# RWKV-7 attention and a SiLU MLP on one core: chunk 0 inverted alone, the inverse turned by VectorE

## The chip, the core and the metric
The kernel runs on one core of a Trainium2 chip. Time is the device time of one execution in microseconds. The median of six runs of the kernel before is 964.92 us (952.55 to 973.38). Engines are TensorE (PE), VectorE (DVE), ScalarE (ACT), GpSimd (POOL) and SyncE (SP). Each engine works through its own list of instructions in order; an instruction that waits holds all behind it. DMA transfers are issued from SP's list and ScalarE's list.

## What is computed
For 4 batches, 8 heads, 768 steps and 40 channels per head a state of 40 by 40 is read, decayed and updated at every step; the result goes through an MLP with SiLU.

```python
for t in range(S):
    y[:, :, t] = np.einsum('bhd,bhde->bhe', rt, state)
    Sa = np.einsum('bhde,bhe->bhd', state, at)
    state = state * wt[:, :, None, :] - np.einsum('bhd,bhe->bhde', Sa, bt)
    state = state + np.einsum('bhd,bhe->bhde', vt, kt)
x = y.transpose(0, 2, 1, 3).reshape(B * S, H * D)      # 3072 x 320
h = x @ w_in                                           # 320 x 2048
out = (h / (1 + exp(-h))) @ w_out                      # 2048 x 320
```

## The kernel before
The 768 steps are cut into 12 chunks (NN) of 64 steps (C). A chunk is worked on as two units (NM), each of two batches. Within a chunk the recurrence is a triangular system, so each chunk needs the inverse of a 64x64 triangle for each of 32 (batch, head) pairs. The stages, by the names in the code:

- `load`, `load_w`, `load_rv` fetch a unit's channels: a, kb (b and k side by side), w, then v, r. `load_weights` fetches a piece of the MLP's weights into a room. The weights arrive as 64-bit floats; `weights` converts a piece in five VectorE and three ScalarE instructions (L164 to L176). The first pieces' rooms share the buffers of gts.
- `pre` (`prepare(n)`) has `scale`: scan products of w (L253), their reciprocal (L255), then GpSimd multiplies a and kb by them (L256, L258), and ScalarE sums squares as a check (L261, L262). And `scores`: TensorE makes the pair products of a and b (`between`, L231), VectorE masks them into sb (L239), and sb goes to the DRAM tile md (L274) with one head per partition.
- `inverse` reads md back into mi (L305) for two chunks at once: 64 partitions for the even chunk, 64 for the odd. For each row, one multiply (L310) and one reduction (L316) on VectorE fill XI. For chunks 0 to 3 (`small`) the triangle is cut to blocks of 16 and there are 15 rows; later there are 31 rows on blocks of 32. `back` writes XI to the DRAM tile zd (L323), turns XI within each partition into mi by two copies (ScalarE L325, VectorE L326) and writes that to xd (L327).
- `merge` has `fetch`, which reads blocks from zd (L343) and xd (L347) into XT, with the step in the partition; `first`, which for chunks 0 to 3 begins with `sixteen` (pq L357, the VectorE mask into qq L365, po L371 and L380, VectorE L390) and makes pq L407; and `second` (po L424), the last of the inverse. qq has the buffer of tmp, which the rows of `inverse` use.
- `chain` is a unit's attention: `keys` (pt L473), `right` (pm L231, masked into sk, pr L495), `solve` (pu L517, pw L535), `read` (pl L571, masked into vl L579), `write` (pgy L603, state Gbd L616 and L620, output yx L625, stored in the DRAM tile xs), `turn` (pt L555).
- `moe` reads xs into xt and makes ph (L666, L671), the sigmoid sg (ScalarE L674), gts (VectorE L675) and po (L682).

`weave` mixes lists of such steps, and the scheduler of the framework then sets each engine's order from that. A tile name with bufs=1 is one buffer: its next use waits until the last reader of the use before is done. Eight semaphores serve the DMA transfers in turn, so a transfer's issue waits until the eighth before it has landed.

The part around the change is the run-up: chunks 0 and 1 are prepared (`prepare(0)`, `prepare(1)`), inverted together (`invert(1)`), then chunk 0's chain runs with chunk 0's `first` and `second` before `solve`, and chunk 1's merge between `read` and `write` of chunk 0 (`late`). The w tiles of the first four units lie in tmp, mi and xt besides their own buffer. RHS, Gbd, GT and XT are cleared on GpSimd between `prepare(0)` and `prepare(1)`.

Of the kernel before, what the change touches and what calls it, by code (L numbers as in the profile page):

```python
# [41 lines left out]
def kernel(  # L42
# [39 lines left out]
    for be in range(2):  # L82
# [18 lines left out]
    XI = XIf[:, 0 : 32 * 32].rearrange("p (s t) -> p s t", s=32)  # L101

    w0 = sb.tile([128, Q, C + 1], F32, name="w")
    early = [
        sb.tile([128, 32 * 32], F32, name=x)[:, 0 : Q * (C + 1)].rearrange("p (q t) -> p q t", q=Q)
        for x in ("tmp", "mi", "xt")
    ]
    for w in [w0] + early:
        nc.vector.memset(w[:, :, 0:1], 0.0)
    nc.vector.memset(one, 0.0)  # L110
# [69 lines left out]

    issued = {}

    def in_order(x):

        if "last" in issued:
            info = mybir.DependencyInfo(mybir.DependencyClass.NoSync, mybir.DependencyReason.DATA)
            tc.add_manual_dep(x.ins, issued["last"].name, info, reason="in order")
        issued["last"] = x.ins

    class Unit:  # L190
# [5 lines left out]
        return u  # L196


    def load(u):
        u.a = sb.tile([128, Q, C], F32, name="a", bufs=4)  # L200
        u.kb = sb.tile([128, Q, 2, C], F32, name="kb", bufs=6)
        B2 = slice(2 * u.m, 2 * u.m + 2)

        def part(n, x):
            for be in range(2):
                nc.sync.dma_start(
                    u.kb[:, P * be : P * be + P, n], x[2 * u.m + be, u.n].rearrange("p (q t) -> p q t", q=P)
                )

        nc.sync.dma_start(  # L210
            u.a.rearrange("p (b q) t -> p b (q t)", b=2), aT[B2, u.n].rearrange("b p c -> p b c")
        )
        part(1, bT)
        part(0, kT)

    def load_w(u, at, queue=nc.sync):
        u.w = at
# [30 lines left out]
    def pre(u, md):  # L248
        def scale():
            u.W = sb.tile([128, Q, C + 1], F32, name="W", bufs=6)  # L250
            for be in range(2):
                W, w = (x[:, P * be : P * be + P].rearrange("p q t -> p (q t)") for x in (u.W, u.w))
                nc.vector.tensor_tensor_scan(W, w, one.rearrange("p q t -> p (q t)"), 0.0, ALU.mult, ALU.add)  # L253
            R = u.w[:, :, 1 : C + 1]
            nc.vector.reciprocal(R, u.W[:, :, 1 : C + 1])  # L255
            nc.gpsimd.tensor_tensor(out=u.a, in0=u.a, in1=u.W[:, :, 0:C], op=ALU.mult)  # L256
            for n in (1, 0):
                nc.gpsimd.tensor_tensor(out=u.kb[:, :, n], in0=u.kb[:, :, n], in1=R, op=ALU.mult)  # L258
            junk = sb.tile([128, Q, C], mybir.dt.bfloat16, name="junk")
            c = 2 * (NM * u.n + u.m)  # L260
            nc.scalar.activation(out=junk, in_=R, func=AF.Square, accum_out=chk[:, c : c + 1])  # L261
            nc.scalar.activation(out=junk, in_=u.W[:, :, 1 : C + 1], func=AF.Square, accum_out=chk[:, c + 1 : c + 2])  # L262

        def scores():
            if u.m == 0:
                sbs[u.n] = sb.tile([128, NM, 2, P, C], F32, name="sb", bufs=2)
            between(u, 1, sbs[u.n][:, u.m])

            M = slice(u.m, u.m + 1) if u.n < 2 else slice(0, NM)
            for be in range(2 if u.n < 2 or u.m == NM - 1 else 0):  # L270
                for c in range(2):
                    at = 64 * (u.n % 2) + 16 * (2 * be + c)
                    r = C * be + 32 * c
                    nc.sync.dma_start(  # L274
                        md[at + 8 * M.start : at + 8 * M.stop].rearrange("q s t -> s q t"),
                        sbs[u.n][r : r + 32, M, :, :, 32 * c : 32 * c + 32].rearrange("s m j p t -> s (m j p) t"),
                    )
            k = NM * u.n + u.m + 1
            if 3 < k < NM * NN:
                load_w(units[k // NM][k % NM], w0)  # L280

        return [scale, scores]

    def small(n):
        return n < 4

    def inverse(md, N, queue):
        steps = []  # L290
        xd = dr.tile([128, 32, 32], F32, name="xd", bufs=2)
        zd = dr.tile([128, 32, 32], F32, name="zd", bufs=2)
        mif = sb.tile([128, 2 * SKIP], F32, name="mi")
        mi = mif[:, 0 : 32 * 32].rearrange("p (s t) -> p s t", s=32)
        I = 32 // N
        tmp = sb.tile([128, 32 * 32], F32, name="tmp")[:, 0 : I * N * N]
        tmp = tmp.rearrange("p (i s t) -> p i s t", i=I, s=N)

        def blocks(x):
            x = x.rearrange("p (i x) -> p i x", x=SKIP)[:, :, 0 : 16 * 32] if N == 16 else x[:, 0 : 32 * 32].unsqueeze(1)  # L300
            return x.rearrange("p i (s t) -> p i s t", t=32)

        X, M = blocks(XIf), blocks(mif)
        for h in range(2):
            nc.sync.dma_start(mi[64 * h : 64 * h + 64], md[64 * h : 64 * h + 64])  # L305

        def row(t):
            n = N - 1 - t
            part = tmp[:, :, 0:n, 0:n]
            nc.vector.tensor_tensor(  # L310
                out=part,
                in0=X[:, :, t + 1 : N, t + 1 : N],
                in1=M[:, :, t, t + 1 : N].unsqueeze(2).to_broadcast([128, I, n, n]),
                op=ALU.mult,
            )
            last = nc.vector.tensor_reduce(out=X[:, :, t + 1 : N, t], in_=part, axis=AX.X, op=ALU.add)  # L316
            mark["row"] = last.ins

        for t in reversed(range(N - 1)):
            steps.append(partial(row, t))  # L320

        def back():
            nc.sync.dma_start(zd, XI)  # L323
            turned = XI.rearrange("p t s -> p s t")
            nc.scalar.copy(out=mi[:, 0:16], in_=turned[:, 0:16])  # L325
            nc.vector.tensor_copy(out=mi[:, 16:32], in_=turned[:, 16:32])  # L326
            queue.dma_start(xd, mi)  # L327

        steps.append(back)
        return steps, xd, zd  # L330

    def merge(n, xd, zd, queue):
        X = XT[n % 2].rearrange("p m h t -> p (m h) t")
        N = NM * H
        box = {}
# [1 line left out]
        def fetch():  # L337
            for be in range(2):
                at = 64 * (n % 2) + 32 * be
                for c in range(2):  # L340
                    r = C * be + 32 * c
                    if c == 0 or small(n):
                        nc.sync.dma_start(  # L343
                            X[r : r + 32, :, 32 - 32 * c : 64 - 32 * c],
                            zd[at + 16 * c : at + 16 * c + 16].rearrange("q t s -> t q s"),
                        )
                    queue.dma_start(  # L347
                        X[r : r + 32, :, 32 * c : 32 * c + 32],
                        xd[at + 16 * c : at + 16 * c + 16].rearrange("q s t -> s q t"),
                    )  # L350

        def sixteen(s, pp):

# [360 lines left out]
            md[0] = dr.tile([128, 32, 32], F32, name="md", bufs=2)  # L714
        return [x for u in units[n] for x in pre(u, md[0])]

    def invert(n):

        if n >= NN or n % 2 == 0:
            return []  # L720
        box = {}
        queue = nc.scalar if n == 1 else nc.sync

        def begin():
            box["rows"], box["xd"], box["zd"] = inverse(md[0], 16 if small(n) else 32, queue)

        def do(k, i):
            if i == 0:
                box[k] = merge(k, box["xd"], box["zd"], queue)
            box[k][i]()  # L730

        late[n - 1] = [partial(do, n, 1), partial(do, n, 2)]
        return (
            [begin]
            + [lambda i=i: box["rows"][i]() for i in range(16 if small(n) else 32)]
            + [partial(do, n - 1, 0), partial(do, n, 0), partial(do, n - 1, 1), partial(do, n - 1, 2)]
        )

    def run(steps):
        for step in steps:  # L740
            step()

    for u, at in zip(units[0] + units[1], [w0] + early):
        load_w(u, at, nc.scalar)
        load(u)
    for n in range(5):
        load_weights(n, nc.scalar)
    convert = [partial(weights, n) for n in range(NW + 1)]

    xs = dr.tile([DM, 4 * NM * C], F32, name="xs", bufs=2)  # L750
    run(prepare(0))
    for t in RHS + Gbd + GT + XT:
        nc.gpsimd.memset(t, 0.0)
    run(prepare(1))
    steps = invert(1)
    run(steps[0:1])
    for u in units[0]:
        load_rv(u)
    chains = {0: [chain(u, xs) for u in units[0]]}
    run([x[i] for i in range(2) for x in chains[0]])  # L760
    run(convert[0:6] + steps[1:16])
    queue = []
    with tc.issue_after(mark["row"]):
        for u in units[2]:
            load(u)
        run(steps[16:])
        steps = [x for pair in zip(*[x[2:] for x in chains[0]]) for x in pair]
        steps[4:4] = late.pop(0)
        weave(steps, convert[6:21])
        for u in units[1]:  # L770
            load_rv(u)
        for u in units[3]:
# [187 lines left out]
```

## Time and profile before
| what | us |
|---|---|
| median of six runs | 964.92 |
| lowest, highest | 952.55, 973.38 |
| the profiled execution | 966.44 |
| its span (first to last instruction) | 964.7 |
| TensorE busy | 838.0 |
| VectorE busy | 532.1 |
| ScalarE busy | 289.7 |
| GpSimd busy | 97.1 |

The mean granted clock of TensorE is 0.906 of full speed. The profiled execution is 1.5 us above the median of the runs, and 1.7 us of it lie outside its span. In the lines below, a time in square brackets is how long the engine was idle before the instruction, and after the arrow stands what ended the wait. A group "x8" is eight instructions of one kind, and its duration runs from the first start to the last end. SPq and ACTq are the lists that issue transfers.

### The profile page before, as it was taken

The page shows a single profiled execution, that of the slowest core. Times are in us where ns is not written, and L with a number is a line of the kernel's source. Part 1 is how long each engine was busy: PE and PEld are TensorE (multiplying, and loading weights), DVE is VectorE, ACT ScalarE, POOL GpSimd, SP SyncE. Part 2 cuts the span into 40 slices and gives each one's busy share as a digit, 9 for nine tenths or more (in the row PEclk, how much of TensorE's full clock was granted, in tenths as well). Part 3 has the DMA queues.
Part 4 walks back from the last instruction along what each step waited for, and adds up shares of the span by engine and source line. Part 5 has one row for each costly group of instructions (what it writes and reads, how often), then busy time and mean ns, then how long its engine had stood idle before and what let it go on. Part 6 is the DMA issues. An engine that isn't in the chain of part 4 may idle for free.

```text
span 964.7 us, 26553 instructions
## 1 busy us (share of the span) xinstructions
PE 838.0 (87%) x11586; PEld 590.5 (61%) x11586; DVE 532.1 (55%) x1078; ACT 289.7 (30%) x660; POOL 97.1 (10%) x98
## 2 busy tenths in 40 slices
PE   0407899789989848999989999979999999999997
PEld 0407887556768723786645876627866468756544
DVE  8955588992106499146894167981549813031111
ACT  2435474522323112235212433113431133210110
POOL 5210010310001101002010012100020000000000
PEclk9855598799659669999999999999999999999999
DMA  9594556433114360355533365313542223002001
GB/s 229 112 233 115 138 153 157 114 84 88 47 38 115 82 150 12 77 141 118 119 76 77 84 149 125 84 31 86 129 96 74 95 48 76 2 8 67 1 1 30
DMA packets 235498, 88.30 MB, mean 92 GB/s; under 512 B 198640, under 2 KB 226544, under 8 KB 235376
## 3 DMA queue, kind: packets, MB, share of 16 engines
q1 hardware_dynamic: 225920, 83.14, 36.1%
q10 hardware_dynamic: 9456, 3.41, 1.7%
q8 instruction: 92, 1.51, 0.6%
q14 instruction: 30, 0.25, 0.1%
HBM read 69.21 MB, written 17.30 MB: 90 GB/s over the span
## 4 chain that ended last, share of the span: by engine, by line
PE 55%; DVE 31%; DMA 4%; issue 4%; SPq 2%; ACT 1%; POOL 1%; ACTq 0%; POOLq 0%; DVEq 0%
PE po L682 15%; PE ph L666 10%; DVE tmp L310 6%; DVE XI L316 6%; PE pl L571 5%; PE ph L671 4%; DVE w L255 3%; DVE W L253 3%; PE pq L407 3%; PE po L424 2%; PE pu L517 2%; DVE gts L675 2%; PE pm L231 2%; PE pr L495 2%; PE pt L473 2%
## 5 line engine op out<-in xcount | busy, mean ns | idle before, releaser
L682 PE MATMUL po<-wo_s,gts 128*128 128x320 f32 x768 | 225.0, 445 | 0.5 <-DVE gts L675 0.4
L666 PE MATMUL ph<-xt,wi_s 128*128 128x512 f32 (+1 forms) x448 | 195.4, 572 | 30.9 <-DVE gts L675 14.8
L682 PEld LDWEIGHTS po<-wo_s,gts 128*128 128x128 f32 x768 | 143.1, 192 | 62.0 <-issue 4.1
L666 PEld LDWEIGHTS ph<-xt,wi_s 128*128 128x128 f32 x448 | 83.1, 199 | 116.1 <-issue 57.7
L675 DVE TENSOR_TENSOR gts<-ph,sg 128x512 f32<-128x512 f32 (+1 forms) x112 | 65.8, 608 | 138.2 <-ACT sg L674 138.1
L674 ACT ACTIVATE sg<-ph 128x512 f32<-128x512 f32 (+1 forms) x112 | 54.8, 533 | 237.0 <-PE ph L671 236.9
L231 PE MATMUL pm<-a,kb 64*64 64x64 f32 x1536 | 48.7, 242 | 39.1 <-POOL kb L258 24.1
L310 DVE TENSOR_TENSOR tmp<-XI,mi 128x2 f32<-128x2 f32 (+35 forms) x154 | 77.5, 503 | 3.5
L258 POOL TENSOR_TENSOR kb<-kb,w 128x512 f32<-128x512 f32 x42 | 50.7, 1228 | 263.8 <-DVE w L255 195.1
L316 DVE TENSOR_REDUCE XI<-tmp 128x2 f32<-128x2 f32 (+35 forms) x154 | 71.6, 465 | 3.8
L231 PEld LDWEIGHTS pm<-a,kb 64*64 64x64 f32 x1536 | 39.8, 149 | 51.3 <-POOL kb L258 42.4
L239 DVE TENSOR_TENSOR sk<-pm,ms 128x256 f32<-128x256 f32 x48 | 18.1, 419 | 95.6 <-PE pm L231 95.5
L255 DVE RECIPROCAL w<-W 128x512 f32<-128x512 f32 x21 | 70.3, 3347 | 0.8
L671 PE MATMUL ph<-xt,wl_s 64*128 64x512 f32 (+1 forms) x224 | 63.2, 604 | 0.0
L256 POOL TENSOR_TENSOR a<-a,W 128x512 f32<-128x512 f32 x24 | 28.8, 1199 | 287.1 <-DMA a<-in_aT 203.3
L571 PEld LDWEIGHTS pl<-r,vut 64*128 64x128 f32 x768 | 52.3, 213 | 4.8 <-issue 2.1
L571 PE MATMUL pl<-r,vut 64*128 64x64 f32 x768 | 53.7, 299 | 1.3 <-DVE vl L579 1.2
L564 ACT COPY GT<-pt 40x512 f32<-40x512 f32 x44 | 25.5, 579 | 87.1 <-PE pt L555 86.5
L579 DVE TENSOR_TENSOR vl<-pl,ml 128x512 f32<-128x512 f32 x48 | 30.9, 685 | 24.3 <-PE pl L571 24.3
L239 DVE TENSOR_TENSOR sb<-pm,ms 128x256 f32<-128x256 f32 x48 | 18.1, 412 | 46.2 <-PE pm L231 46.1
L603 PE MATMUL pgy<-vl,kt 128*64 128x104 f32 (+1 forms) x768 | 41.9, 267 | 0.0
L671 PEld LDWEIGHTS ph<-xt,wl_s 64*128 64x128 f32 x224 | 19.2, 195 | 35.2 <-issue 34.0
(106 smaller groups left out, 1016.8 us busy)
## 6 DMA issues: line engine op xcount, KB each, us to landing
a<-in_aT SPq DMA_DIRECT2D x24, 256.0 KB
kb<-in_bT SPq DMA_DIRECT2D x48, 128.0 KB
kb<-in_kT SPq DMA_DIRECT2D x48, 128.0 KB
vut<-in_vT SPq DMA_DIRECT2D x48, 128.0 KB
r<-in_rT SPq DMA_DIRECT2D x24, 256.0 KB
w<-in_wT SPq DMA_DIRECT2D x40, 128.0 KB
room<-in_w_out SPq DMA_DIRECT2D x20, 256.0 KB
v<-in_v SPq DMA_DIRECT2D x48, 80.0 KB
```

The source lines that it names most:

```text
L231: nc.tensor.matmul(pm[j][C * be : C * be + C, p * C : p * C + C], lhsT=u.kb[J, q, n, :], rhs=u.a[J, q, :], start=True, stop=True,)
L255: nc.vector.reciprocal(R, u.W[:, :, 1 : C + 1])
L258: nc.gpsimd.tensor_tensor(out=u.kb[:, :, n], in0=u.kb[:, :, n], in1=R, op=ALU.mult)
L310: nc.vector.tensor_tensor(out=part, in0=X[:, :, t + 1 : N, t + 1 : N], in1=M[:, :, t, t + 1 : N].unsqueeze(2).to_broadcast([128, I, n, n]) ...
L316: last = nc.vector.tensor_reduce(out=X[:, :, t + 1 : N, t], in_=part, axis=AX.X, op=ALU.add)
L571: nc.tensor.matmul(pl[j][:, q * C : q * C + C], lhsT=u.vut[J, q].rearrange("p n t -> p (n t)"), rhs=u.r[J, q, :], start=True, stop=True,)
L603: nc.tensor.matmul(pgy[be][J, p * N + last * D : p * N + N], lhsT=u.kt[:, P * be + p, J], rhs=u.vl[:, P * be + p, j, last * D :], start=u. ...
L666: in_order(nc.tensor.matmul(ph[n], lhsT=wi_s[:, k, at : at + 128], rhs=xt[:, k, :], start=k == 0, stop=False))
L671: in_order(nc.tensor.matmul(ph[n], lhsT=wl_s[R, i, :], rhs=xt[R, 2, :], start=False, stop=True))
L674: nc.scalar.activation(out=sg, in_=ph[n], func=AF.Sigmoid)
L675: nc.vector.tensor_tensor(out=place(2 * i + n), in0=ph[n], in1=sg, op=ALU.mult)
L682: in_order(nc.tensor.matmul(po[:, 0:DM], lhsT=place(f)[:, b * 128 : b * 128 + 128], rhs=wo_s[:, NF // 2 * half + f, :], start=f == 0, stop ...
```

## The change
1. `inverse` takes partitions lo to hi. Chunk 0 is inverted alone in 64 partitions (`invert(0, 1)`) and then chunk 1 alone (`invert(1, 1)`); later chunks still go in pairs. Chunk 1's rows are issued after chunk 0's `second`, and its `first` and `second` come after `write` of chunk 0 and before `turn` (`steps[6:6]` for `steps[4:4]`).
2. zd is gone. `fetch` reads xd alone, and a 32x32 block transpose on VectorE makes the other orientation within XT: four per chunk for chunks 0 to 3, two per chunk later.
3. Clearing RHS, Gbd, GT and XT comes first on GpSimd.
4. Order and queues: md of chunks 0 and 1 is written by ScalarE's queue, once per chunk (8 transfers for 16), chunk 1's after mi of chunk 0 is issued. The first weight pieces come from SP behind the loads of chunks 0 and 1; b and k of chunk 2 are loaded earlier. For chunk 0 the k product on GpSimd and the check sums come after the scores (`keys`), and scans and reciprocals stay in program order. Four weight pieces are converted among chunk 0's rows, for six before.
5. The w tiles of the first units lie in buffers of sg and xt.

```diff
+    def behind(x, ins):
+        info = mybir.DependencyInfo(mybir.DependencyClass.NoSync, mybir.DependencyReason.DATA)
+        tc.add_manual_dep(x.ins, ins.name, info, reason="in order")
...
-            for n in (1, 0):
-                nc.gpsimd.tensor_tensor(out=u.kb[:, :, n], in0=u.kb[:, :, n], in1=R, op=ALU.mult)
+            nc.gpsimd.tensor_tensor(out=u.kb[:, :, 1], in0=u.kb[:, :, 1], in1=R, op=ALU.mult)
+            if u.n > 0:
+                keys()
...
-            M = slice(u.m, u.m + 1) if u.n < 2 else slice(0, NM)
-            for be in range(2 if u.n < 2 or u.m == NM - 1 else 0):
+            queue = nc.scalar if u.n < 2 else nc.sync
+            for be in range(2 if u.m == NM - 1 else 0):
...
+                    if u.n == 1:
+                        behind(x, mark["mi"])
...
-        for h in range(2):
-            nc.sync.dma_start(mi[64 * h : 64 * h + 64], md[64 * h : 64 * h + 64])
+        for h in range(lo, hi, 64):
+            mark["mi"] = queue.dma_start(mi[h : h + 64], md[h : h + 64]).ins
+        L = slice(lo, hi)
...
-            nc.sync.dma_start(zd, XI)
...
-                    if c == 0 or small(n):
-                        nc.sync.dma_start(
-                            X[r : r + 32, :, 32 - 32 * c : 64 - 32 * c],
-                            zd[at + 16 * c : at + 16 * c + 16].rearrange("q t s -> t q s"),
-                        )
...
+            for r in range(0, 128, 32 if small(n) else 64):
+                c = r % 64
+                nc.vector.transpose(out=X[r : r + 32, :, 32 - c : 64 - c], in_=X[r : r + 32, :, c : c + 32])
...
+    for t in RHS + Gbd + GT + XT:
+        nc.gpsimd.memset(t, 0.0)
     for u, at in zip(units[0] + units[1], [w0] + early):
         load_w(u, at, nc.scalar)
-        load(u)
-    for n in range(5):
-        load_weights(n, nc.scalar)
-    convert = [partial(weights, n) for n in range(NW + 1)]
-
-    xs = dr.tile([DM, 4 * NM * C], F32, name="xs", bufs=2)
-    run(prepare(0))
-    for t in RHS + Gbd + GT + XT:
-        nc.gpsimd.memset(t, 0.0)
-    run(prepare(1))
-    steps = invert(1)
-    run(steps[0:1])
+    for n in range(2):
+        for what in "ab", "k":
+            for u in units[n]:
+                load(u, what)
+    for n in range(3):
+        load_weights(n)
     for u in units[0]:
         load_rv(u)
+    for n in range(3, 5):
+        load_weights(n)
+    for u in units[2]:
+        load(u, "bk")
+    convert = [partial(weights, n) for n in range(NW + 1)]
+
+    xs = dr.tile([DM, 4 * NM * C], F32, name="xs", bufs=2)
+    steps = prepare(0)
+    run([steps[i] for i in (0, 3, 1, 4, 2, 5)])
+    rows = invert(0, 1)
+    run(rows[0:1])
+    run(prepare(1))
     chains = {0: [chain(u, xs) for u in units[0]]}
     run([x[i] for i in range(2) for x in chains[0]])
-    run(convert[0:6] + steps[1:16])
+    run(convert[0:4] + rows[1:17])
     queue = []
     with tc.issue_after(mark["row"]):
+        run(rows[17:])
+        rows = invert(1, 1)
+        run(late.pop(0))
+        run(rows)
         for u in units[2]:
-            load(u)
-        run(steps[16:])
+            load(u, "a")
         steps = [x for pair in zip(*[x[2:] for x in chains[0]]) for x in pair]
-        steps[4:4] = late.pop(0)
-        weave(steps, convert[6:21])
+        steps[6:6] = late.pop(1)
+        weave(steps, convert[4:21])
```

## The prediction
> **What bounds the kernel now.** I read the slices of the page first, then the table by windows, the timelines of TensorE and VectorE, and the chain of waits for the first 130 us.
>
> ```profile
> PE   0407899789989848999989999979999999999997
> DVE  8955588992106499146894167981549813031111
> PEclk9855598799659669999999999999999999999999
> ```
>
> A slice is 24.1 us. From about 385 us on TensorE is at 9 nearly everywhere: what is to be won lies before. Three places show it idle: the first 72 us, a loose stretch up to 220 us, slice 14.
>
> ```profile
> 53.00:73.00 20.00, 0.53 (x4) 0.35 (x4) 10.44 (x24) 7.92 (x22) 3.63 (x3) 0.50 1.01 217
> 89.00:103.00 14.00, 13.91 (x216) 13.71 (x219) 5.31 (x16) 9.18 (x25) 0.00 (x0) 0.50 0.56 140
> 170.00:195.00 25.00, 19.38 (x155) 12.90 (x154) 24.77 (x45) 13.04 (x35) 6.73 (x6) 0.80 0.51 121
> ```
>
> Columns: length; busy TensorE, weight load, VectorE, ScalarE, GpSimd; granted clock, DMA share, GB/s. In 53 to 73 us TensorE does nothing while the inverse travels through DRAM. At 170 to 195 us VectorE is full (24.77 of 25) and TensorE has holes.
>
> ```profile
> 37.32 3.85 DMA mi<-md
> 53.89 4.35 DMA xd<-mi
> ...
> 60.77 4.81 DMA kb<-in_bT
> 66.28 5.28 DMA room<-in_w_in
> ```
> ```profile
> 69.06 4.05 SPq L343 DMA_DIRECT2D XT<-zd  x8
> 78.23 0.48 DVE L365 TENSOR_SCALAR qq<-pq,lower 128x256 f32<-128x256 f32 x1
> 124.88 1.67 PE L555 MATMUL pt<-ident,Gbd 64*40 64x64 f32 x32 [0.95 <-DVE Gbd L620]
> 185.68 1.14 PE L231 MATMUL pm<-a,kb 64*64 64x64 f32 x32 [4.49 <-POOL kb L258]
> 187.76 2.07 PE L666 MATMUL ph<-xt,wi_s 128*128 128x256 f32 x4 [0.94 <-DVE gts L675]
> 356.42 5.73 PE L666 MATMUL ph<-xt,wi_s 128*128 128x512 f32 x8 [13.46 <-DMA xt<-xs]
> ```
>
> The scores come back at 41.2 us, 15 rows run to 52.7 us, xd lands at 58.2, but zd is issued only at 64.27 behind loads that wait on SP; its eight reads start at 69.06. The first step with the inverse on VectorE (L365) is at 78.23. From 124.88 us (the state turned, chunk 1 begins) to 220.6 us, where chunk 3's inverse is done, MoE work runs between the chunks.
>
> **The change, part by part.** The order of each engine's instructions in the changed program gives what stands behind what.
>
> 1. *Start and chunk 0's rows.* Per unit the same scan, reciprocal (3.3 us) and products are done. Memsets of some 5 us move ahead of GpSimd's products, where it idled 5.48 us: nothing. The six weight transfers leave the ScalarE queue for SP behind all loads, md (8 transfers for 16) leaves SP for ScalarE. At the start's 229 GB/s the 4.2 MB of channels and 0.8 MB of weights are in by 23 us, 1.7 MB of r and v by 31 us. Reciprocals end at about 10.8, 17.6, 23.8, 29.3 us (before: 30.0); md's four writes wait for the second unit's mask at 24.5 us. But mi<-md stands on ScalarE behind two key copies, which need TensorE after the fourth score: 34.2 us, landing near 38 (before: 41.2). Then chunk 0's first row stands on VectorE behind the second unit's sk, which needs pr of the first: 39.6 us. Chunk 1's four md writes wait on ScalarE for loads of SP until about 38.5 us; behind them stand only copies that are needed from 40 us on. Gain 1.7 us. Nine weight conversions (0.33 us apart: 3.0) now stand among the rows and one sk mask less: rows end at 53.7 instead of 52.7. Half the partitions save nothing, the row is as long.
>
> 2. *The way back.* xd is issued at 55.5 (after the copy, 1.07), lands at about 58.3 (128 KB; 2.3 to 4.4 us by xd's 4.35 under a full DMA). ScalarE issues four XT reads in place of eight, landed by 64. zd's write (6) and its 32 reads go away. In their place stand the transposes, four per merge, 32x512 each. No row has one; VectorE's copy of 512 columns (L326) takes 0.58. The Trainium skill speaks against it: "VectorE: DVE Perf Modes", section "The three transpose paths", has 311 ns for a 128x128 bf16 tile, so an estimate of 4 x 311 = 1.24 us for 512 columns. By the row four cost 2.4 us, by the rule 5.0, on the path for chunks 0 and 1: the sum is up to 5.2 us worse. I take 0.6, the nearest row (bounds 0.5 and 1.24); below nothing is excluded, it is added work. They stand behind ten conversions and chunk 2's scan and reciprocal (1.3 + 3.35) on VectorE: start 65.7, end 69.2; with 2.3 us of matmuls and six conversions L365's successor runs at 71.7. Gain **6.5 us**. The 16 + 16 later transposes stand where VectorE idles (19.88 us behind chunk 5's rows): nothing; without that cover 0.6 each, 14 us at most over the rest.
>
> 3. *Chunk 1 inverted on its own.* Fifteen more rows of two instructions: 41.3 to 52.7 less 0.75 of mask, 10.7 us on VectorE. Their tmp is the buffer of chunk 0's qq, so the first row waits for chunk 0's last merge matmul: 88.4 - 6.5 = 82 us. Between the rows stand 16 conversions (0.28 each: 4.5), four vl masks (2.6) that wait for pl (96.3), Gbd's and yx's updates (5.9): rows end at about 105. Then conversions (3), chunk 2's second scan and reciprocal (4.65) are still ahead of the transposes, so X is ready near 119, while xd and four reads (2.8 + 4 + 2) hide behind them. TensorE has pgy done at 99.6 and waits 20 us in order. Next is the merge, 14.3 us in the trace (102.76 to 117.09), plus 1.7 as a reciprocal of chunk 3 stands before its L390: the turn at 135 instead of 124.9. **+10 us**; with a transpose of 1.24, +13.
>
> 4. *What that wait buys.* VectorE meanwhile does chunk 2's second and chunk 3's two reciprocals (before at 135, 169 and 181 us), at an equal count of converted weights (21). The stretch to 220 us had TensorE waiting 4.49 + 0.94 us there, and 3.2 us of half-clock matmuls after it (L666 x4 took 2.07, 1.13 warm). That goes: -8.6. Of other stalls in the stretch (1.20 and 1.17 us behind VectorE, 3.0 of cold matmuls after the first) I count half: -2.7. Sum **-11.3 us**, bounds -5 and -16.
> The skill's rule on the clock ("TensorE: Matmul & The Clock Gate", Part 1: full rate after some 3.4 us of sustained work) would let denser solving at 67 to 99 us double its speed, -10 us more. The row 89.00:103.00 denies it: 13.91 of 14 us busy, clock 0.50. These small matmuls don't lift it; I count nothing there.
>
> 5. *Slice 14.* TensorE waits 13.46 us for xt<-xs, whose yx stands behind a reciprocal. In the changed TensorE order one 16-matmul po group of the MoE before and two ph matmuls come after the last turn of chunk 3, so they run in this hole: 16 x 0.29 + 0.5 = **-5.1 us** (bounds 0 and -8). The later order is nearly the same: nothing.
>
> Sum: -6.5 is spent inside +10; +10 - 11.3 - 5.1 = -6.4. Against the profiled execution (966.44 us, span 964.7) 960; the median of the runs is 1.5 lower than that execution, so 958.5; said as 959.
>
> **Rivals.**
> - *A, as summed* (0.47): chunk 1 late, given back by VectorE's slack and the filled hole. 954 to 964.
> - *B, larger gain* (0.27): VectorE is the true bound from 125 to 220 us. For: 91.91 of 103 us busy at 117 to 220, reciprocals on the chain of waits. Three gone with their scans are 14 us, and if conversions cost less among rows, X of chunk 1 comes 4 earlier: -6.4 - 4 - 4 = 952. Against: TensorE too is at 90.93 of 103.
> - *C, slower* (0.12): the second inversion is the bound. Its place is TensorE's queue at the first pq of chunk 1; +10 stays, relief only 5 and the hole as wide as before: 965 + 5 = 970; with transposes at the rule's price 973 to 976. It decides once X of chunk 1 is ready after some 128 us instead of 119. For: the tmp wait and 37 us of VectorE work between 82 and 119 in strict order.
> - *D, nothing gained* (0.14): each wait is taken over by the next, 963 to 967. The transposes may also not replace a wait: XT<-xd was there by 68 us, and the conversions kept VectorE to 78 anyway.
>
> **How the numbers follow.** 1% (9.6 us, about what tells a change from none here) is 955 and 974. Faster by more: most of B and a part of A's low end: 0.34. Slower by more: C's upper half and a little more: 0.09. The same: 0.57. The range takes A, most of B, D and C's lower part: 947 to 971.
>
> **What would show it.** Right: chunk 0's first row at 38 to 41 us, its transposes near 0.6 us and over by 70; L365's successor at 70 to 74; TensorE idle some 20 us before chunk 1's pq, VectorE busy then; no 4.49 us hole behind GpSimd near 185; the hole before xt<-xs under 10 us. Wrong: X of chunk 1 before 105 us (gain over 1%); transposes at 1.2 us; the clock at 1.0 in 70 to 100 us; VectorE waiting on XT reads in later chunks with gts queued behind.

## The result, and the profile after

| | before | after |
|---|---|---|
| median, first comparison | 964.72 us (37 runs) | 955.29 us (16 runs) |
| lowest, highest | 952.55, 976.72 | 949.11, 964.34 |
| profiled execution, its span | 966.44, 964.7 | 959.11, 957.0 |

The ratio is 0.9936 with a 95% interval of 0.9911 to 0.9960: 0.64% faster, inside the 1% that was said; the median is 3.7 us under the 959 us. The ratio takes only the fast runs of both kernels, those within 1.5% of the kernel's fastest, so it is not the quotient of the two medians (0.9902). A second comparison (run e11) gave 0.9865 (0.9821 to 0.9910), which is outside that 1%. The two intervals do not meet, so one comparison is less certain than its interval says. The change gains between half and one and a half per cent. The total came out as forecast; of its terms two did not, with opposite signs, and that the sum came so near is in part luck.

The slices of the changed kernel (tenths of busy time; PEclk is the granted clock):

```profile
PE   0518378989999979999989999989999999999996
...
DVE  8797888896226796264993367971649723031120
...
PEclk9855559889979999997999999999999999999999
```

Slices are counted from 0. TensorE's hole in slice 14 is smaller (7 for 4). PEclk was 6, 5, 6 and 6 in slices 10, 11, 13 and 14; now it is 9, 7, 9 and 9, and below 9 behind that only in slice 18 (7). The stretches that the prediction showed, in the columns it explained:

```profile
53.00:73.00 20.00, 3.42 (x186) 3.05 (x188) 19.61 (x45) 8.64 (x22) 4.53 (x5) 0.50 0.71 171
89.00:103.00 14.00, 14.00 (x179) 13.76 (x178) 11.19 (x31) 6.98 (x21) 0.00 (x0) 0.52 0.32 80
170.00:195.00 25.00, 24.71 (x333) 18.28 (x335) 22.62 (x54) 10.10 (x26) 2.20 (x2) 0.92 0.57 144
```

At 53 to 73 us VectorE is full (19.61 for 10.44) and TensorE has begun. At 89 to 103 us TensorE is as full as before and the clock still half. At 170 to 195 us VectorE is relieved (22.62 for 24.77) and TensorE has no large hole (24.71 for 19.38). In order of time:

```profile
40.64 0.15 DVE L316 TENSOR_TENSOR tmp<-XI,mi 64x2 f32<-64x2 f32 x1 [0.43 <-DMA mi<-md]
...
64.83 1.38 DVE L353 STREAM_TRANSPOSE XT<-XT 32x512 f32<-32x512 f32 x2
...
71.71 0.48 DVE L368 TENSOR_SCALAR qq<-pq,lower 128x256 f32<-128x256 f32 x1
...
84.00 0.16 DVE L316 TENSOR_TENSOR tmp<-XI,mi 64x2 f32<-64x2 f32 x1 [0.70 <-PE po L427]
...
123.75 0.71 DVE L353 STREAM_TRANSPOSE XT<-XT 32x512 f32<-32x512 f32 x1
```
```profile
121.74 0.25 PE L360 MATMUL pq<-XT,sb 16*32 16x16 f32 x2 [18.21 <-DVE XT L353]
...
138.20 3.64 PE L558 MATMUL pt<-ident,Gbd 64*40 64x64 f32 x64
...
184.07 0.68 PE L230 MATMUL pm<-a,kb 64*64 64x64 f32 x16 [0.29 <-ACT GT L567]
...
205.47 2.08 PE L669 MATMUL ph<-xt,wi_s 128*128 128x256 f32 x4 [2.77 <-DVE gts L678]
...
332.34 5.11 PE L685 MATMUL po<-wo_s,gts 128*128 128x320 f32 x18 [1.17 <-DVE gts L678]
339.89 3.70 PE L669 MATMUL ph<-xt,wi_s 128*128 128x512 f32 x8 [2.44 <-DMA xt<-xs]
```

The lines show chunk 0's first row (40.64), the transposes (0.70 us each), the first qq (71.71, before 78.23), and chunk 1's rows behind the last merge matmul (84.00). Then TensorE waits 18.21 us for chunk 1's inverse, and the state turns at 138.2 us. The hole of 4.49 us behind GpSimd near 185 us is 0.29; the one before xt<-xs, 13.46 us, is left as 1.17 and 2.44.

**Where the time went.** The page's rows of TensorE for before, after, and after once more (run e11):

```profile
PE 838.0 (87%) x11586; PEld 590.5 (61%) x11586; DVE 532.1 (55%) x1078; ACT 289.7 (30%) x660; POOL 97.1 (10%) x98
```
```profile
PE 830.8 (87%) x11586; PEld 585.8 (61%) x11586; DVE 567.4 (59%) x1141; ACT 291.2 (30%) x661; POOL 97.9 (10%) x98
```
```profile
PE 821.9 (87%) x11586; PEld 576.7 (61%) x11586; DVE 566.4 (60%) x1141; ACT 291.1 (31%) x661; POOL 97.6 (10%) x98
```

Span less busy time is TensorE's idle time: 964.7 - 838.0 = 126.7, 957.0 - 830.8 = 126.2, 948.3 - 821.9 = 126.4 us. It is the same. What fell is busy time for the same 11586 matmul records. The clock accounts for it: four ph matmuls took 2.07 us at half clock and 1.13 us at full clock, and with half of the time at half clock (122.6, 103.6 and 83.3 us) taken off, 776.7, 779.0 and 780.3 us of busy time are left. Cut at the same work, the second MoE stage's first po matmul (219.77 us before, 232.89 after), and with the clock record laid over the matmuls:

| us | idle, up to there | behind | busy at half clock, up to there | behind |
|---|---|---|---|---|
| before | 77.6 | 49.1 | 60.7 | 61.9 |
| after | 89.7 | 36.4 | 62.7 | 41.0 |
| after again | 88.9 | 37.6 | 62.8 | 20.5 |

The start gave 12 us of idle time more and the rest took it back; half of the fall in half-clock time (122.6 to 103.6 us: 9.5) is about what the shown execution won (7.7 of span). Between the two executions of the changed kernel, 8.7 us apart, hardly anything but the clock differs. The timed runs agree: their mean clock is 0.907 before (67 runs) and 0.922 after (20), and among the 67 the time and the mean clock of a run have a correlation of -0.93. A correlation shows no cause by itself; e5 below tests it.

### The profile page after: what moved, and what is told of

Same layout as the page of the kernel before. It is cut to its first block, busy times and chain, and to the rows that moved or that the text cites. A ratio compares the mean times of both kernels' runs of the same rounds, so it can differ in the third digit from the quotient of the medians.

```text
span 957.0 us, 26541 instructions
## 1 busy us (share of the span) xinstructions
PE 830.8 (87%) x11586; PEld 585.8 (61%) x11586; DVE 567.4 (59%) x1141; ACT 291.2 (30%) x661; POOL 97.9 (10%) x98
## 4 chain that ended last, share of the span: by engine, by line
PE 55%; DVE 31%; DMA 6%; issue 4%; SPq 2%; ACT 2%; POOL 1%; ACTq 0%; POOLq 0%; DVEq 0%
PE po L685 13%; PE ph L669 10%; DVE tmp L316 7%; DVE XI L322 6%; PE pl L574 5%; PE ph L674 3%; DVE w L255 3%; PE pq L410 3%; PE pu L520 3%; PE pt L476 2%; DVE gts L678 2%; PE pgy L606 2%; PE pr L498 2%; PE pm L230 2%; PE po L427 2%
## 5 line engine op out<-in xcount | busy, mean ns | idle before, releaser
L685 PE MATMUL po<-wo_s,gts 128*128 128x320 f32 x768 | 222.3, 442 | 3.1 <-DVE gts L678 3.0
L669 PE MATMUL ph<-xt,wi_s 128*128 128x512 f32 (+1 forms) x448 | 196.0, 572 | 21.4 <-DVE gts L678 17.6
L677 ACT ACTIVATE sg<-ph 128x512 f32<-128x512 f32 (+1 forms) x112 | 54.6, 533 | 232.6 <-PE ph L674 232.3
L316 DVE TENSOR_TENSOR tmp<-XI,mi 64x2 f32<-64x2 f32 (+40 forms) x169 | 80.9, 479 | 7.9 <-DMA mi<-md 3.5
L255 DVE RECIPROCAL w<-W 128x512 f32<-128x512 f32 x24 | 80.3, 3346 | 1.1
L322 DVE TENSOR_REDUCE XI<-tmp 64x2 f32<-64x2 f32 (+40 forms) x169 | 76.3, 452 | 4.0
L230 PEld LDWEIGHTS pm<-a,kb 64*64 64x64 f32 x1536 | 37.7, 143 | 43.5 <-POOL kb L257 33.3
L257 POOL TENSOR_TENSOR kb<-kb,w 128x512 f32<-128x512 f32 x24 | 29.1, 1213 | 290.1 <-DVE w L255 199.4
L582 DVE TENSOR_TENSOR vl<-pl,ml 128x512 f32<-128x512 f32 x48 | 31.1, 685 | 29.3 <-PE pl L574 29.2
L360 PE MATMUL pq<-XT,sb 16*32 16x16 f32 x512 | 9.0, 195 | 45.2 <-DVE XT L353 44.3
L254 DVE TENSOR_TENSOR_SCAN W<-w,one 128x260 f32<-128x260 f32 x48 | 35.1, 750 | 9.8 <-DMA w<-in_wT 9.8
```

The lines of the kernel that those rows point to most:

```text
L230: nc.tensor.matmul(pm[j][C * be : C * be + C, p * C : p * C + C], lhsT=u.kb[J, q, n, :], rhs=u.a[J, q, :], start=True, stop=True,)
L254: pin(nc.vector.tensor_tensor_scan(W, w, one.rearrange("p q t -> p (q t)"), 0.0, ALU.mult, ALU.add))
L255: pin(nc.vector.reciprocal(R, u.W[:, :, 1 : C + 1]))
L316: nc.vector.tensor_tensor(out=part, in0=X[L, :, t + 1 : N, t + 1 : N], in1=M[L, :, t, t + 1 : N].unsqueeze(2).to_broadcast([hi - lo, I, n, ...
L322: last = nc.vector.tensor_reduce(out=X[L, :, t + 1 : N, t], in_=part, axis=AX.X, op=ALU.add)
L669: in_order(nc.tensor.matmul(ph[n], lhsT=wi_s[:, k, at : at + 128], rhs=xt[:, k, :], start=k == 0, stop=False))
```

## The experiments

The table has all kernels: the ratio to the kernel before, the mean clock of the timed runs (runs whose records lack the slow first 100 us left out), and from the one profile of each the first matmul of chunk 1's turn, the first po of the second MoE stage and TensorE's idle time (e10's profile is not read here). e1 to e4, e5 to e8, and e9 to e12 were timed together, beside runs of the kernel before. The same kernel in two such comparisons came out 0.7% (after and e11) and 0.6% (e6 and e12) apart, so differences of that size between comparisons are not told apart.

| run | ratio (95%) | clock | turn | po | idle |
|---|---|---|---|---|---|
| before | 1 | 0.907 | 122.2 | 219.8 | 126.7 |
| after | 0.9936 (0.9911 to 0.9960) | 0.922 | 138.2 | 232.9 | 126.2 |
| e1 together | 0.9894 (0.9867 to 0.9921) | 0.913 | 124.4 | 223.4 | 125.8 |
| e2 turn only | 0.9989 (0.9966 to 1.0013) | 0.906 | 114.3 | 218.3 | 115.2 |
| e3 qq apart | 0.9938 (0.9905 to 0.9971) | 0.911 | 127.4 | 225.2 | 124.6 |
| e4 zd back | 0.9968 (0.9939 to 0.9998) | 0.914 | 130.3 | 232.3 | 125.5 |
| e5 before, filled | 0.9899 (0.9829 to 0.9969) | 0.922 | 122.5 | 222.3 | 126.7 |
| e6 after, filled | 0.9836 (0.9779 to 0.9894) | 0.926 | 139.4 | 239.2 | 125.9 |
| e7 e1, filled | 0.9938 (0.9900 to 0.9977) | 0.919 | 124.2 | 219.9 | 125.5 |
| e8 e7, warm start | 0.9827 (0.9774 to 0.9880) | 0.941 | 125.4 | 219.9 | 97.0 |
| e9 before, held | 0.9943 (0.9906 to 0.9981) | 0.915 | 122.6 | 220.9 | 125.0 |
| e10 e7, held | 0.9946 (0.9898 to 0.9994) | 0.912 | - | - | - |
| e11 after again | 0.9865 (0.9821 to 0.9910) | 0.926 | 137.4 | 232.2 | 126.4 |
| e12 e6 again | 0.9898 (0.9852 to 0.9943) | 0.923 | 135.9 | 235.1 | 126.9 |

**e1: chunks 0 and 1 inverted together again.**

```diff
-                    if u.n == 1:
-                        behind(x, mark["mi"])
...
-    rows = invert(0, 1)
-    run(rows[0:1])
     run(prepare(1))
+    rows = invert(1)
+    run(rows[0:1])
...
-        rows = invert(1, 1)
-        run(late.pop(0))
-        run(rows)
...
-        steps[6:6] = late.pop(1)
+        steps[6:6] = late.pop(0)
```

> The changed kernel with chunks 0 and 1 inverted together again; turning on VectorE, clearing and queue order stay. Theory W (my prediction's step 4: what the wait for chunk 1's own inverse costs is won back because VectorE works ahead meanwhile): chunk 1 turns near 118 us instead of 138.3, but the holes at 170 to 220 us behind GpSimd and VectorE come back, and TensorE's idle time behind 140 us rises from 45 us towards the 61 us of before; 951 to 958 us. Rival P (the second inversion is a pure price, the later gain comes from the other edits): the 16 us of idle time go and nothing comes back, 938 to 946 us, idle time of TensorE near 110 us in the whole instead of 126.

The turn came 14 us earlier, less than the 20 expected: the joint mi stood on ScalarE behind chunk 1's md, and the first row waited 7.97 us for it. The ratio is 0.4% under that of after in the first comparison and 0.3% above its second: not told apart. P is out: it wanted 9 to 17 us less than after's 955, and the idle time is 125.8 us, not 110. W, from 4 us less than after to 3 more, takes the ratio in, and the idle time behind 140 us rose from 45.2 to 55.8 us as W said. But it did not come back where W said, at 170 to 220 us (holes of 1.9, 1.4, 1.3 and 1.0 us): the hole before xt<-xs is 12.93 us, as in before, and 28 us of matmuls ran at half clock between 223 and 297 us, 13.7 in after for the same stretch of work.

**e2: transposes alone, on the kernel before.** zd's tile, its write and its reads go out, the two transpose lines of the diff come in.

> The kernel before with one part of the change alone: the second DRAM trip (zd) gives way to transposes on VectorE; order of loads and the joint inversion of chunks 0 and 1 stay. My step 2: the first qq on VectorE comes at 70 to 74 us instead of 78.2, 957 to 961 us. Rival D (the trip was hidden: XT<-xd lands by 68 us anyway and conversions hold VectorE): first qq at 76 to 79 us, 963 to 967 us. Transposes 0.6 to 0.7 us each in both.

The view of VectorE in order of time:

```profile
61.43 1.42 DVE L346 STREAM_TRANSPOSE XT<-XT 32x512 f32<-32x512 f32 x2
...
69.70 0.46 DVE L361 TENSOR_SCALAR qq<-pq,lower 128x256 f32<-128x256 f32 x1
```

The first qq is at 69.70, 8.5 us early: in this order of transfers the zd trip was not hidden, against rival D, and the profile has 11.5 us less idle time. Yet the ratio is 0.9989. The turn is 8 us early, the second MoE stage 1.4, and the half-clock time went from 122.6 to 140.8 us, which costs 9. So D's end, no gain, came true by another way. What step 2 says of the trip holds in the kernel before, and is worth nothing there on its own.

**e3: chunk 1's rows freed from chunk 0's qq.**

```diff
-            both = sb.tile([128, N, 48], F32, name="qq", tag="tmp")
+            both = sb.tile([128, N, 48], F32, name="qq", tag="tmp" if n else "xt")
```

> The changed kernel with chunk 0's qq in another buffer than the rows' tmp, so that chunk 1's rows need not wait for chunk 0's last merge matmul (they began at 84.0 us). Both theories: rows begin near 70 us and end by 95, TensorE's wait before chunk 1's first pq falls from 18.2 to under 8 us. Theory P (the wait is a price): the time falls by 8 to 14 us, 941 to 948 us. Theory W (the wait buys VectorE's lead): half or less of it stays, 950 to 956 us.

Rows began at 70.4 us (and ended at 99.6, not by 95), TensorE waited 6.07 us instead of 18.21, the turn came 11 us earlier, and the ratio did not move (0.9938). The 11 us are 7.7 at the second MoE stage, and by the third turn (299.8 us for 287.0) the kernel stands behind after. Between the second MoE stage and the fourth turn 50.9 us of its matmuls ran at half clock, 17.1 in after. Theory W's range (950 to 956 us) took in the unchanged time; P is out: the wait that chunk 1 was given is no price at the end.

**e4: the zd trip back in the changed kernel** (the reverse of e2's edit).

> The changed kernel with the second DRAM trip (zd written, read by strided DMAs) in place of the transposes; all else stays. My step 2: chunk 0's first qq 5 to 7 us later than 71.7 us, and the time up by 3 to 7 us, 958 to 962 us. Rival D (the trip is hidden behind conversions in either order): within 2 us of the changed kernel, 953 to 957 us.

```profile
53.52 0.50 SPq L330 DMA_DIRECT2D zd<-XI  x1
...
67.20 0.47 DVE L372 TENSOR_SCALAR qq<-pq,lower 128x256 f32<-128x256 f32 x1
...
111.94 0.26 PE L364 MATMUL pq<-XT,sb 16*32 16x16 f32 x2 [13.58 <-DMA XT<-zd]
```

Both theories missed the first qq: with the trip back it comes at 67.20 us, 4.5 us before the 71.71 of after, where step 2 said 5 to 7 us later. In this order SP issues zd at 53.52 us, as soon as the rows are done, where the kernel before had it at 64.27; the transposes of after start only at 64.83, behind a reciprocal on VectorE. Chunk 1's turn comes 8 us earlier too (130.3 us). None of it is left at the second MoE stage (232.3 us for 232.9), and the ratio is 0.9968, against the 0.9936 and 0.9865 of after. Behind that stage idle time is 40.1 us for 36.4, and time at half clock 49.3 for 41.0. So the transposes may be worth something, but not by the earlier start that step 2 counted on; by what, isn't shown.

**e5 to e7: TensorE's holes filled.** In `sixteen`, for chunks 2 and 3 (`WARM`), three matmuls stand behind each of two groups:

```diff
+        def warm(out, last):
+            if n not in WARM:
+                return None
+            for i in range(3):
+                x = nc.tensor.matmul(
+                    out[:, 256:512], lhsT=ident, rhs=one.rearrange("p q t -> p (q t)")[:, 0:256], start=True, stop=True
+                )
+                behind(x, last.ins)
+                last = x
+            return last
```

> The kernel before with twelve more matmuls (identity by a constant, 128x256, written to an unused half of a PSUM bank and never read) put into TensorE's holes in the merges of chunks 2 and 3: three behind each group of 16x16 pq matmuls and three behind each following po group. Work is only added. Theory C (what sets the time behind 220 us is TensorE's granted clock, which falls to half for some 17 us after a hole of about 1 us in these merges; the kernel before spent 35.4 us of matmul time at half rate between 220 and 298 us): that falls below 15 us, the mean clock over the timed runs rises from 0.907 to 0.915 or more, the time falls by 5 to 10 us, ratio 0.990 to 0.995. Rival N (the clock is no cause, the holes are set by VectorE anyway): the added work costs 0 to 4 us, ratio 1.000 to 1.004, clock unchanged.

> The changed kernel with the same twelve matmuls. Its profiled execution spent only 13.7 us at half rate in this stretch. Theory C: 2 to 5 us less than the changed kernel, ratio 0.988 to 0.992, clock 0.925 to 0.935. Rival N: 0 to 4 us more, ratio 0.994 to 0.998.

> The changed kernel with chunks 0 and 1 inverted together (ratio 0.9894 on its own) and the same twelve matmuls in the merges of chunks 2 and 3. Theory C: its 28 us at half rate between 223 and 297 us fall below 12, the ratio to 0.982 to 0.986. Rival N: 0.989 to 0.993.

The stretch of these merges in before, and in e5:

```profile
220.00:300.00 80.00, 74.15 (x1567) 58.37 (x1567) 16.23 (x41) 20.09 (x47) 4.43 (x6) 0.77 0.30 69
300.00:345.00 45.00, 37.74 (x690) 32.81 (x689) 25.20 (x45) 13.56 (x31) 6.99 (x6) 0.79 0.44 102
```
```profile
220.00:300.00 80.00, 74.70 (x1647) 58.80 (x1646) 21.96 (x52) 22.23 (x51) 4.44 (x6) 0.89 0.31 72
300.00:345.00 45.00, 31.01 (x647) 26.08 (x645) 30.68 (x66) 13.45 (x33) 9.31 (x8) 0.90 0.56 128
```

In the first row 80 more matmul records (24 are the filling) in nearly the same busy time, and a clock of 0.89 for 0.77; at half clock ran 16.5 us of this work, a little over the 15 that C said, for 35.4. On the kernel before, work that nobody reads made it 1.0% faster (0.3 to 1.7), with the same idle time (126.7 us), and the mean clock rose from 0.905 to 0.922: there the clock is a cause. The size is less certain, since two comparisons of one kernel differed by up to 0.7%. It is no recipe. e7 lost where it should have won (37.6 us at half clock in spite of the filling), and e6's gain over after did not come again (e12). Theory C holds for the kernel before and is not shown for the others.

**e8: TensorE kept busy before chunk 0's solve.** This is e7 with the merges of chunks 0 and 1 filled too, and:

```diff
...
+    for i in range(56):
+        x = nc.tensor.matmul(
+            fill[:, 0:256], lhsT=ident, rhs=one.rearrange("p q t -> p (q t)")[:, 0:256], start=True, stop=True
+        )
+        behind(x, last.ins)
+        last = mark["fill"] = x
```

> As the run before, with the merges of chunks 0 and 1 filled too, and 56 such matmuls ahead of chunk 0's first pq, where TensorE idles 25.7 us. The matmuls of chunk 0's solve ran at a clock of 0.50 however busy TensorE was. Theory C: with no idle stretch ahead of it the solve runs at full clock, chunk 1's state turns at 108 to 114 us instead of 124.4. Rival B of the prediction (VectorE is the bound up to 220 us) then says that the MoE's 64th po group still begins within 4 us of the 223.4 us without it, and the ratio is that of the run before within 0.003; if TensorE is the bound there, the time falls by 8 us or more, ratio 0.972 to 0.978. Rival N: the clock stays at 0.50 before 120 us.

```profile
53.00:73.00 20.00, 20.00 (x95) 17.60 (x94) 18.75 (x44) 4.55 (x10) 1.18 (x1) 1.00 0.69 159
73.00:122.00 49.00, 42.64 (x1118) 37.86 (x1116) 34.59 (x93) 23.02 (x61) 4.39 (x6) 0.66 0.38 95
```

Full clock at 53 to 73 us while the filling ran, 0.66 in the solve: its merges have holes of their own, and the turn came no earlier (125.4). So this filling won nothing in this solve; what a solve at full clock would win was not reached. The second MoE stage stayed within 4 us, as rival B says. The ratio fell all the same, which B did not say, with the widest spread of all (946.66 to 977.99 us). In the two profiles the gain over e7 lies behind the second MoE stage: idle time there is 48.1 us for 48.7, and time at half clock 20.4 us for 51.9. What brought the better clock isn't settled.

**e9 and e10: two po groups held back for the hole before xt<-xs.**

```diff
+                if n0 == 1 and half == 1 and f == 0:
+                    behind(x, mark["turn", 3])
```

> The kernel before with one more order on TensorE: the last two po groups of the second MoE stage (32 matmul records, 9 us) may not run before chunk 3's state is turned, so that they stand where the changed kernel has them, in the hole before xt<-xs. Nothing is added or taken away. Theory H (the filled hole is the larger part of the gain behind 220 us): the hole falls from 13.46 us to 3 to 6 us, the work is not missed where it stood, time down by 7 to 10 us, ratio 0.990 to 0.993. Rival M (those groups filled other holes, which open in their place): ratio 0.997 to 1.003, with new idle time of TensorE or time at half clock between 230 and 340 us.

> The changed kernel with chunks 0 and 1 inverted together and twelve filling matmuls (ratio 0.9938 on its own), and the order of the run before. Theory H: 0.984 to 0.988. Rival M: 0.992 to 0.997.

TensorE in e9:

```profile
312.96 1.04 PE L540 MATMUL pw<-XT,RHS 64*64 64x64 f32 x18 [2.10 <-DVE sb L244]
...
318.63 1.13 PE L236 MATMUL pm<-a,kb 64*64 64x64 f32 x32 [4.63 <-POOL kb L263]
...
353.75 5.40 PE L672 MATMUL ph<-xt,wi_s 128*128 128x512 f32 x8 [4.68 <-DMA xt<-xs]
```

The hole fell from 13.46 to 4.68 us, and 2.10 opened in front (4.63 was 4.03). Idle time between the second MoE stage and the fourth turn rose by 6.1 us, and fell by 10.5 from there to the sixth turn; over the whole it fell by 1.6 us. The ratio is 0.57% below 1 (0.2 to 0.9) and lies between both theories, with an interval that touches both. So some of the groups' 9 us may be won, and how much isn't shown. e10 shows no gain over e7, as M said.

**e11 and e12: after and its filled form once more.**

> The changed kernel itself, on this chip beside the others. Ratio 0.991 to 0.996 as on record; clock over the timed runs 0.918 to 0.926. Its profile shows which of the half-clock stretches come again: the one of some 14 us near 259 us, and the one near 440 us that follows a wait of 0.44 us for w.

> The changed kernel with the twelve filling matmuls once more (0.9836 with an interval of 0.978 to 0.989 on few runs), beside the changed kernel on the same chip. Theory C: 0.3 to 1.0 per cent below the changed kernel's ratio of this call, clock higher by 0.003 or more. Rival N: equal or above it.

The changed kernel (after) came out better than at first. In its first profile 13.7 us ran at half clock from 440 us, behind a wait of VectorE of 0.44 us for w and a hole of TensorE of 1.41 us behind GpSimd. Here the wait is gone, the hole is 0.87 us, and the stretch at half clock is gone:

```profile
430.00:456.00 26.00, 24.04 (x354) 19.06 (x352) 11.98 (x19) 6.71 (x17) 3.51 (x3) 0.74 0.37 83
```
```profile
430.00:456.00 26.00, 25.10 (x374) 17.06 (x371) 19.57 (x37) 6.17 (x15) 3.94 (x4) 1.00 0.56 125
```

At half clock 13.7 us cost 6.8. One pair of profiles doesn't prove that the short wait decided it. Of the 13.7 us near 259 us, 10.2 came again.

## Why the prediction was right

1. *Start.* Near, with another last wait. Reciprocals ended at 11.6, 17.5, 24.1 and 30.3 us (10.8, 17.6, 23.8, 29.3 said), mi was issued at 34.80 (34.2), the first row came at 40.64 (39.6), the rows ended at 54.2 (53.7). But the row waited for the scores' transfer (0.43 us), which I had landing near 38, and not for sk, which was done at 40.2; the gain at the first row was 0.7 us for 1.7.
2. *The way back.* The times were right: transposes from 64.83 to 69.66 us (65.7 to 69.2), 0.70 us each, so the copy's row (0.6) was nearer than the estimate from another tile's figure (1.24), and the qq at 71.71 as forecast. What I put the 6.5 us down to was not right: zd's trip cost 8.5 us in the order of the kernel before (e2), where zd is issued at 64.27. In the changed order the qq comes 4.5 us earlier with the trip than with the transposes (e4). So up to the qq the other edits won 11.0 us, the transposes took 4.5 of them back, and the hit is in part luck. And neither 8.5 us in e2 nor 4.5 us in e4 reached the end.
3. *Chunk 1 on its own.* Mechanism right, size off: rows from 84.0 to 109.5 (82 to 105), X ready at 124.5 (119), and a turn at 138.2: 16.0 us after that of before by its first matmul (122.2), where +10 was said. The 5 us by which X was late are a conversion that waited 2.06 us ahead of the first row, rows behind the waits for pl (1.23) and pgy (0.74), and the last transpose behind a conversion (0.62). TensorE waited 18.21 us, near the 20 said. With zd's trip for the transposes the turn is at 130.3 (e4).
4. *What the wait buys.* This failed. The second MoE stage began 13.1 us later, so of the 16.0 only 2.9 came back by then, where -11.3 stood in the sum. The hole that was named is gone (0.29 us at 184.07), but others opened: 2.77 at 205.47, 1.68 at 165.96, 1.79 at 147.72. Between the turn and the second MoE stage idle time fell by 3.3 us (12.1 to 8.7), and time at half clock rose from 13.5 to 18.2, which takes 2.4 back; the other 2 us are not traced. I had taken the holes of one trace off one by one and left the rest as it was.
5. *Slice 14.* Mechanism right, size off by two. The "16 matmuls" were counted in the program's order; the trace has two records for each, and the 0.29 us is that of one record. 32 records ran there (4.04 + 5.11 us, and three pairs of ph at 0.70), and 13.46 became 3.61: 9.9 us for 5.1. In e9 6.1 of 8.8 us opened again where the groups came from. In the changed kernel idle time there fell, from 10.3 to 4.2 us; why isn't shown.
6. *"The later order is nearly the same: nothing."* This failed too, and it held the gain. Behind the second MoE stage the changed kernel won 12.6 us of idle time (9.6 between the fourth and sixth turn) and 10 to 21 by the clock, in the two executions. In the profiled one +13 up to the second MoE stage and -21 behind it stand where the sum had -1 and -5: two errors of 14 and 16 us that nearly cancel. That the total was met is luck to this extent.

On the clock I counted nothing, by the row of 89 to 103 us. For that stretch the zero was right (clock 0.52 after the change), but not the reason, that these small matmuls don't lift it: after five full steps of them the clock rose at 102.4 us (in before four such steps were not enough; last section). It was wrong to stop there. The Trainium skill ("TensorE: Matmul & The Clock Gate", Part 1) says that the window in which the use of TensorE is judged runs freely, so that the same kernel varies from run to run. e11 beside after shows such a variation; that the window is its cause no run here shows.

Left open: which edit brings the better clock. e1, e3 and e4, each the changed kernel with one thing altered, lost some of it (0.913, 0.911 and 0.914 for 0.922), and e2, the kernel before with one part of the change, gained none (0.906). Rival C's cause came near (X of chunk 1 at 124.5 us, its deciding point was 128; relief of 2.9 us for its 5) and its end did not come; B's reason, VectorE as the bound to 220 us, fits e2, whose turn lies 8 us ahead of before and whose second MoE stage only 1.4 (VectorE busy 88.2 of 98 us between 122 and 220, but TensorE 87.1), and e4, whose turn lies 8 us ahead of after and whose second MoE stage 0.6. In e1 and e3, 9.5 and 7.7 us of some 14 and 11 were left at that stage. So B's bound is argued and not shown.

## What to carry to other kernels

A change to the order of a mixed queue is to be summed in two columns, idle time and busy time at the lower clock: here the first came out equal and the second made the result. An earlier start is worth what is left of it at the next common wait, so follow it to there before booking it. What an edit brings in one order of transfers says little of another: taking zd's trip out brought the first qq 8.5 us forward in the kernel before and put it 4.5 us back in the changed one. And when a program's instruction counts are multiplied by a trace's durations, count in the trace's records.

## What the runs showed of the hardware

The clock record changes in steps of 3.41 us. Over 13 profiles (all but that of e7, whose record begins late) I counted, for every such step at full clock, how busy TensorE was and whether the next was at half:

| busy share of the step | steps | followed by half clock |
|---|---|---|
| under 0.40 | 69 | 69 |
| 0.40 to 0.75 | 189 | 53 |
| 0.75 to 0.90 | 177 | 15 |
| 0.90 and over | 2473 | 14 |

So idle time of 0.9 to 2 us in a step (busy 0.40 to 0.75) was enough in 53 of 189 cases. The clock came back mostly after one to five full steps in a row (busy 0.97 and over), but only after eight or nine in e2, e3, e4 and e10, where the stretches from about 260 us on lasted 34 to 38 us. In e2 about a third of that stretch went to matmuls of 32 rows and less. In before four full steps of chunk 0's solve, from 91 to 104 us, did not bring it back. In after it rose at 102.4 us after five, just as TensorE ran out of work:

```profile
84.00:102.00 18.00, 17.37 (x234) 17.17 (x236) 14.40 (x43) 9.99 (x27) 0.00 (x0) 0.50 0.33 89
102.00:106.00 4.00, 1.53 (x27) 1.33 (x23) 3.81 (x11) 0.00 (x0) 0.00 (x0) 0.93 0.48 76
```

The 32x32 transposes of 32x512 fp32 took 0.70 us, where a copy of 512 columns took 0.58.
